# GpSimd is allowed to make the staged weights' sums and low parts in a one-core window attention with two feed-forward layers

## The chip, the cores and the metric

The kernel runs on one core of a Trainium2 chip, as one program. The metric is the device time of one execution in microseconds; lower is better. The engines are named as the profile names them: PE is TensorE (PEld its weight loads), DVE is VectorE, ACT is ScalarE, POOL is GpSimd, SP is SyncE, which here issues every DMA. Each engine works through its own queue of instructions in order, and waits at an instruction until the semaphores that it needs have arrived.

## The reference, cut to what matters

Four sequences of 576 tokens with 8 heads of 64 columns go through causal attention with a window of 64; the result, 2304 tokens by 512 columns, goes through two feed-forward layers with 2048 hidden columns.

```python
scores = scale * np.matmul(q, k.transpose(0, 1, 3, 2))
mask = (rel >= 0) & (rel < window)
...
x = np.ascontiguousarray(attn_out.transpose(0, 2, 1, 3)).reshape(B * S, H * D)
# layer 1
h = x @ w_in
r = np.maximum(h, 0.0)
x = (s * (r * r) + b) @ w_out
# layer 2
h = x @ w_in
g = np.maximum(h, 0.0) + alpha * np.minimum(h, 0.0)
return (g @ w_out).astype(np.float32)
```

## The kernel before

**Numbers in two parts.** A weight or an activation `a` is kept as a high part (a copy to fp32r, `hi`) and a low part (`a - hi`, `lo`), and a product is three matmuls: high by high, high by low, low by high. The function `pair` makes both parts: the copy runs on ACT (in some places DVE may take it), the subtraction on DVE.

**Fewer products.** For most of both layers, two blocks of 128 hidden columns are multiplied together by a scheme with seven block products in place of eight (`hidden_pair`, `product`). It needs, beside the weights themselves, four sums of weight halves. `weight_pair` makes these for the input weights of a pair of hidden blocks, and `out_pair` makes the like for four pairs of output weights: each converts two weight blocks from the 64-bit input (`converted`: ACT lines 668 and 672, DVE lines 677 to 687), makes four sums of 128x256 (`adds`, lines 765 to 768 and 1133 to 1136, into the tile `as__86`), and calls `pair` on the blocks and on the sums. A row with the name `raw` as input is a converted block, one with `as__86` a sum.

**Staging.** Two of the 13 input pairs are written straight into the weight area `aw` (`direct`). The other 11, and all four output pairs, are made ahead of time in the tiles `ag` (now and then `as__86`), stored to the DRAM tensors `wd` and `vd` (SP lines 788 and 1148) and loaded again when their turn comes (lines 809 and 1115). Inputs `x` go the same way through `xd` (stores line 823, loads line 941).

**What PE does with it.** A pair's seven products share PSUM banks: product 1 writes bank `h`, ACT copies it to a bank of `ab` (line 989), product 6 goes on in that copy, which is copied again for product 7, and once more into an `h` bank for product 4. PE has projections (line 1419, `y`) to do between these, and the order in PE's queue is fixed. If a copy is late, PE stands still at the next dependent product.

**What sets the order.** The class `Plan` records every piece of work as a step with the engines that may do it, an assumed cost for each, what it reads and writes, and a due time. `emit` then plays the steps through with these assumed costs, picks for each step the engine on which it would end soonest (weighted by `SPARE`), and issues instructions in that order. An order once issued is fixed; on the chip only the semaphores decide when an instruction starts. The assumed costs of this case:

```python
def act(cols, fn):
    return ("act", 0.2 + cols * 0.00084, fn, 0.0)
...
def dve(cols, fn, fast=False, port=False):
    return ("dve", 0.15 + cols * (0.00053 if fast else 0.00106), fn, 0.0) + (True,) * (fast or port)
...
def pool(cols, fn):
    return ("pool", 0.1 + cols * 0.00184, fn, 0.0)
```

A DVE step with the fifth entry `True` is charged 0.8 of the time by which it would overlap a POOL step.

Of the kernel before, what the change touches and what calls it, by code (L numbers as in the profile page):

```python
# [58 lines left out]
def f32(ap):  # L59
    return ap.bitcast(F32)  # L60
# [188 lines left out]
def tile_window_attention_two_mlps(  # L249
# [74 lines left out]
# [5 lines that stand above are left out]
# [28 lines left out]
    with tc.manual_schedule():  # L357
# [334 lines left out]
        def pair(cols, src, hi, lo, reads, keys, at, after=0.0, either=True):  # L692

            ways = [act(cols, lambda: nc.scalar.copy(hi(), src()))]
            if either == 2 or either and at < PAIRS_ACT:
                ways.append(dve(cols, lambda: nc.vector.tensor_copy(hi(), src()), fast=True))
            T.step(ways, reads=reads, writes=[k + "h" for k in keys], at=at, after=after)
            T.step(
                [dve(cols, lambda: nc.vector.tensor_sub(lo(), src(), f32(hi())), port=True)],  # L699
                reads=reads + [k + "h" for k in keys], writes=[k + "l" for k in keys], at=at, after=after,  # L700
            )
# [54 lines left out]
        def weight_pair(n, layer, f1, f2, at, after, direct):  # L756
# [7 lines left out]
            def adds():  # L764
                nc.vector.tensor_add(sv(0), a(1, 0), a(1, 1))
                nc.vector.tensor_sub(sv(2), a(0, 0), a(1, 0))
                nc.vector.tensor_sub(sv(1), sv(0), a(0, 0))
                nc.vector.tensor_sub(sv(3), a(0, 1), sv(1))
# [3 lines left out]
            def stage(k, s, reads):  # L772
# [11 lines left out]
                pair(cols, s, lambda: v(0), lambda: v(1), reads, keys, at, after)  # L784
# [8 lines left out]
            T.step([("dve", 1.75, adds, 0.0, True)], reads=ts, writes=[sums_], at=at, after=after)  # L793
# [326 lines left out]
        def out_pair(k, at, after):  # L1120
# [11 lines left out]
            def adds():  # L1132
                nc.vector.tensor_add(sv(0), a(1, 0), a(1, 1))
                nc.vector.tensor_sub(sv(2), a(0, 0), a(1, 0))
                nc.vector.tensor_sub(sv(1), sv(0), a(0, 0))
                nc.vector.tensor_sub(sv(3), a(0, 1), sv(1))
# [3 lines left out]
            def stage(lo, hi, s, reads):  # L1140
# [5 lines left out]
                pair(cols, s, lambda: half(0), lambda: half(1), reads, [key], at, after)  # L1146
# [8 lines left out]
            T.step([("dve", 1.75, adds, 0.0, True)], reads=ts, writes=[sums_], at=at, after=after)  # L1155
# [519 lines left out]
```

## Time and profile before

| what | value |
|---|---|
| median of three runs | 842.25 us (841.49 to 843.48) |
| the profiled execution | 840.98 us, of which the span is 839.2 us |
| PE, PEld busy | 824.7 us (98%), 775.7 us (92%) |
| DVE, ACT, POOL busy | 693.1 us (83%), 536.9 us (64%), 106.1 us (13%) |
| granted TensorE clock | 1.0 throughout |

The span runs from the first to the last instruction. Busy times are sums over one engine's instructions; since matmuls are pipelined, a short pause between two of them does not show as idle time of PE, and the idle time of PEld is the better measure of it.

### The profile page before, as it was taken

The numbers are of one execution on the slowest core, as the hardware profiler recorded it, in microseconds if no ns is written. First come the engines' busy times: TensorE is split into PE (matmuls) and PEld (weight loads), VectorE is DVE, ScalarE is ACT, GpSimd is POOL, SyncE is SP. The second block draws the span as 40 slices with busy tenths as digits, with TensorE's granted clock in tenths as the row PEclk, the third lists the DMA queues.
The fourth block names the chain that finished last, engine by engine and source line by source line (L and its number), as shares of the span: only waits on it lengthen the run. The fifth ranks groups of instructions, "written<-read, shape, count | busy, mean of one in ns | idle before, by whom it ended". The sixth has DMA issues, their size and how long they took to land.

```text
span 839.2 us, 15002 instructions
## 1 busy us (share of the span) xinstructions
PE 824.7 (98%) x5517; PEld 775.7 (92%) x5521; DVE 693.1 (83%) x1210; ACT 536.9 (64%) x1219; POOL 106.1 (13%) x117
## 2 busy tenths in 40 slices
PE   8899999999999999999999999999999999999997
PEld 4678878888899999999999999999999999999997
DVE  6978799698987887699888999878888688778695
ACT  6878997554676555477648678778655345445461
POOL 6443344442011010011000000000000000000000
PEclk9999999999999999999999999999999999999999
DMA  8576974467558989958799668858998667438813
GB/s 287 183 229 176 297 222 131 184 235 284 212 204 314 376 312 316 411 186 339 282 382 380 227 248 309 320 183 303 345 389 314 230 225 268 123 121 338 319 42 109
DMA packets 72648, 217.25 MB, mean 259 GB/s; under 512 B 7424, under 2 KB 25984, under 8 KB 72576
## 3 DMA queue, kind: packets, MB, share of 16 engines
q1 hardware_dynamic: 72576, 216.31, 71.8%
q8 instruction: 43, 0.70, 0.3%
q14 instruction: 29, 0.24, 0.1%
HBM read 151.00 MB, written 65.27 MB: 258 GB/s over the span
## 4 chain that ended last, share of the span: by engine, by line
PE 76%; DVE 10%; DMA 6%; ACT 3%; POOL 3%; issue 1%; SPq 0%; DVEq 0%; POOLq 0%; ACTq 0%
PE y L1419 23%; PE h L978 17%; PE ab L978 13%; PE y L1218 11%; DMA raw<-w_in 3%; PE h L1336 3%; DMA xd<-aq 3%; PE y L1396 3%; PE y L628 2%; PE y L597 2%; PE ab L523 1%; DVE aq L699 1%; ACT as__86 L562 1%; POOL as__86 L580 1%; DVE ag L1051 1%
## 5 line engine op out<-in xcount | busy, mean ns | idle before, releaser
L1419 PE MATMUL y<-ax,woh 128*128 128x384 f32 x864 | 196.2, 334 | 0.0
L978 PE MATMUL h<-ax,aw 128*128 128x384 f32 x936 | 184.4, 334 | 0.7 <-ACT h L989 0.6
L978 PEld LDWEIGHTS h<-ax,aw 128*128 128x128 f32 x936 | 164.2, 188 | 1.6 <-ACT h L989 0.9
L1419 PEld LDWEIGHTS y<-ax,woh 128*128 128x128 f32 x864 | 153.7, 188 | 0.5 <-DVE ay L1496 0.3
L978 PE MATMUL ab<-ax,aw 128*128 128x384 f32 x702 | 139.7, 335 | 1.1 <-ACT h L989 0.9
L978 PEld LDWEIGHTS ab<-ax,aw 128*128 128x128 f32 x702 | 123.1, 188 | 2.4 <-ACT h L989 1.6
L1419 PE MATMUL y<-ax,wol 128*128 128x384 f32 x432 | 121.2, 334 | 0.0
L1336 PE MATMUL h<-ax,aw 128*128 128x512 f32 (+1 forms) x360 | 83.9, 377 | 1.1 <-DVE ax L646 1.1
L1419 PEld LDWEIGHTS y<-ax,wol 128*128 128x128 f32 x432 | 79.0, 188 | 0.0
L1336 PEld LDWEIGHTS h<-ax,aw 128*128 128x128 f32 x360 | 62.0, 189 | 12.8 <-DVE ax L646 1.5
L1051 DVE TENSOR_TENSOR ax<-r,ax 128x384 fp32r<-128x384 f32 x108 | 57.9, 553 | 5.7 <-ACT ax L1048 5.2
L668 ACT ACTIVATE raw<-raw 128x512 f32<-128x512 f32 x64 | 43.2, 679 | 28.8 <-DMA raw<-w_in 16.5
L1006 DVE TENSOR_TENSOR aq<-ab,aq 128x768 f32<-128x768 f32 x39 | 37.3, 955 | 15.7 <-PE ab L978 11.9
L1062 ACT ACTIVATE r<-r 128x384 f32<-128x384 f32 (+2 forms) x90 | 47.5, 543 | 1.1
L580 POOL TENSOR_TENSOR as__86<-as__86,den 128x512 f32<-128x512 f32 x36 | 40.3, 1142 | 56.2 <-DVE den L573 34.1
L682 DVE SCALAR_TENSOR_TENSOR raw<-raw 128x512 int32<-128x512 int32 x64 | 46.3, 725 | 1.2 <-ACT raw L672 1.2
L1058 ACT ACTIVATE r<-h 128x384 f32<-128x384 f32 (+2 forms) x57 | 29.7, 521 | 27.4 <-PE h L1336 17.6
L1499 DVE TENSOR_TENSOR ay<-y,ay 128x384 f32<-128x384 f32 x72 | 37.7, 553 | 9.6 <-PE y L1419 9.5
L733 POOL TENSOR_TENSOR wsum<-wsum,raw 128x512 f32<-128x512 f32 x15 | 21.9, 1459 | 181.6 <-DVE raw L687 180.1
L687 DVE CUSTOM_DVE_ANT_0 raw<-raw 128x1024 uint16<-128x1024 uint16 x64 | 44.7, 704 | 0.1
L672 ACT ACTIVATE raw<-raw 128x512 int32<-128x512 uint32 x64 | 43.0, 680 | 2.4 <-DMA raw<-w_in 1.6
L1218 PE MATMUL y<-ax,woh 128*128 128x384 f32 (+1 forms) x183 | 41.3, 333 | 0.6 <-ACT y L1232 0.6
(164 smaller groups left out, 1493.7 us busy)
## 6 DMA issues: line engine op xcount, KB each, us to landing
ax<-xd SPq DMA_DIRECT2D x91, 768.0 KB, 6.3
aw<-wd SPq DMA_DIRECT2D x33, 512.0 KB, 5.1
raw<-w_in SPq DMA_DIRECT2D x32, 512.0 KB, 6.9
raw<-w_out SPq DMA_DIRECT2D x32, 512.0 KB, 5.5
xd<-ax SPq DMA_DIRECT2D x21, 768.0 KB, 4.5
wd<-ag SPq DMA_DIRECT2D x30, 512.0 KB, 6.6
xd<-aq SPq DMA_DIRECT2D x12, 768.0 KB, 4.1
xd<-ax SPq DMA_DIRECT2D x36, 192.0 KB, 4.6
```

Source lines behind the costliest of these rows:

```text
L580: eng.tensor_mul(x, x, d)
L668: [act(512, lambda: nc.scalar.activation(T[t], H().bitcast(F32), AF.Abs, scale=65536.0))],
L672: [act(512, lambda: nc.scalar.activation(L(), L().bitcast(U32), AF.Copy, scale=2.0 ** -29))],
L682: [dve(512, lambda: nc.vector.scalar_tensor_tensor(out=L(), in0=H(), scalar=-0x80000000, in1=L(), op0=ALU.bitwise_and, op1=ALU.bitwise_or) ...
L687: [dve(512, lambda: nc.vector.tensor_tensor(ti(), ti(), L(), op=ALU.add), port=True)],
L978: nc.tensor.matmul(bank(), W[:, wj, a, kt * P:(kt + 1) * P], X[:, c, kt, :], start=start and kt == 0 and y == 0, stop=kt == 1 and y == 2, ...
L1051: [dve(n, lambda: nc.vector.tensor_sub(T[gl], rn(), f32(T[gh])), port=True)],
L1062: [act(n, lambda: nc.scalar.activation(rn(), rn(), AF.Square)), dve(n, lambda: nc.vector.tensor_mul(rn(), rn(), rn()), port=True)],
L1218: nc.tensor.matmul(v(to)[:, c], W[:, s, a * P:(a + 1) * P], G[:, h, c], start=start and p == 0 and y == 0, stop=p == 1 and y == 2, skip_gr ...
L1336: nc.tensor.matmul(T[ps][:, :n].rearrange("p (c t) -> p c t", t=P), T[w][:, k * P:(k + 1) * P], T[X(x, k)], start=st, stop=sp,)
L1419: nc.tensor.matmul(ps, T[w][:, m * P:(m + 1) * P], T[x], start=(i == 0 and j == 0), stop=(last and j == 2), skip_group_check=closing(layer ...
L1499: ways = [dve(n, lambda a=a, yn=yn: nc.vector.tensor_add(a(), yn(), a()))]
```

## The change

`pair` gets an argument `spare`; where it is true, the low part may also be made by GpSimd. `weight_pair` sets it for staged pairs, `out_pair` always, and in both the four sums may be made by GpSimd too, at an assumed cost of 2.4 us for all four against 1.75 us on DVE. Nothing is computed differently; which engine takes a step is decided by `emit`.

```diff
-        def pair(cols, src, hi, lo, reads, keys, at, after=0.0, either=True):
+        def pair(cols, src, hi, lo, reads, keys, at, after=0.0, either=True, spare=False):
...
             T.step(
-                [dve(cols, lambda: nc.vector.tensor_sub(lo(), src(), f32(hi())), port=True)],
+                [dve(cols, lambda: nc.vector.tensor_sub(lo(), src(), f32(hi())), port=True)]
+                + [pool(cols, lambda: nc.gpsimd.tensor_sub(lo(), src(), f32(hi())))] * spare,
...
-            def adds():
-                nc.vector.tensor_add(sv(0), a(1, 0), a(1, 1))
-                nc.vector.tensor_sub(sv(2), a(0, 0), a(1, 0))
-                nc.vector.tensor_sub(sv(1), sv(0), a(0, 0))
-                nc.vector.tensor_sub(sv(3), a(0, 1), sv(1))
+            def adds(eng):
+                eng.tensor_add(sv(0), a(1, 0), a(1, 1))
+                eng.tensor_sub(sv(2), a(0, 0), a(1, 0))
+                eng.tensor_sub(sv(1), sv(0), a(0, 0))
+                eng.tensor_sub(sv(3), a(0, 1), sv(1))
...
-                pair(cols, s, lambda: v(0), lambda: v(1), reads, keys, at, after)
+                pair(cols, s, lambda: v(0), lambda: v(1), reads, keys, at, after, spare=not direct)
...
-            T.step([("dve", 1.75, adds, 0.0, True)], reads=ts, writes=[sums_], at=at, after=after)
+            T.step([("dve", 1.75, lambda: adds(nc.vector), 0.0, True)] + [("pool", 2.4, lambda: adds(nc.gpsimd), 0.0)] * (not direct),
+                   reads=ts, writes=[sums_], at=at, after=after)
...
-                pair(cols, s, lambda: half(0), lambda: half(1), reads, [key], at, after)
+                pair(cols, s, lambda: half(0), lambda: half(1), reads, [key], at, after, spare=True)
...
-            T.step([("dve", 1.75, adds, 0.0, True)], reads=ts, writes=[sums_], at=at, after=after)
+            T.step([("dve", 1.75, lambda: adds(nc.vector), 0.0, True), ("pool", 2.4, lambda: adds(nc.gpsimd), 0.0)],
+                   reads=ts, writes=[sums_], at=at, after=after)
```

The issued order shows which instructions moved. Counted over the program, 123 instructions leave DVE for POOL: 41 low parts of 128x512 (two times 256 columns), 22 low parts of 128x256, and 60 sums of 128x256 (four each for 11 input pairs and 4 output pairs). Beside these, a handful of small steps change between ACT and DVE. PE has the same 4941 matmuls and SP the same 440 DMAs as before. The order of every engine is the same up to about the first staged pair and, for PE, again over its last 1050 or so matmuls. Line numbers of the changed kernel are higher by 1 from line 700, by 2 from line 795 and by 3 from line 1158.

First, DVE at the first staged input pair, before; line 699 is a low part, 765 to 768 the four sums, 1051 a low part of an activation that PE will read:

```order
L687 ISA raw<-raw 128x1024
L699 TENSOR_TENSOR ag<-raw,ag 128x2x256
L765 TENSOR_TENSOR as__86<-raw 128x256
L766 TENSOR_TENSOR as__86<-raw 128x256
L767 TENSOR_TENSOR as__86<-as__86,raw 128x256
L768 TENSOR_TENSOR as__86<-raw,as__86 128x256
L1051 TENSOR_TENSOR ax<-r,ax 128x384
L1006 TENSOR_TENSOR aq<-ab,aq 128x768
L1051 TENSOR_TENSOR ax<-r,ax 128x384
L699 TENSOR_TENSOR ag<-as__86,ag 128x2x256 x2
```

The same place on DVE in the change:

```order
L687 ISA raw<-raw 128x1024
L682 SCALAR_TENSOR_TENSOR raw<-raw 128x512
L1053 TENSOR_TENSOR ax<-r,ax 128x384
L687 ISA raw<-raw 128x1024
L1053 TENSOR_TENSOR ax<-r,ax 128x384
L1008 TENSOR_TENSOR aq<-ab,aq 128x768
L1061 TENSOR_SCALAR r<-aq 128x384
L742 SCALAR_TENSOR_TENSOR wol_2966<-raw,s_sb,woh_2954 128x512
```

The low parts and sums are gone from DVE, and conversion and activation work closes up. On POOL, where there was a run of `wsum` additions before, the change has, at the first staged pairs:

```order
L700 TENSOR_TENSOR ag<-raw,ag 128x2x256
L766 TENSOR_TENSOR as__86<-raw 128x256
L767 TENSOR_TENSOR as__86<-raw 128x256
L768 TENSOR_TENSOR as__86<-as__86,raw 128x256
L769 TENSOR_TENSOR as__86<-raw,as__86 128x256
L734 TENSOR_TENSOR wsum<-wsum,raw 128x512
L700 TENSOR_TENSOR ag<-as__86,ag 128x2x256 x2
L700 TENSOR_TENSOR ag<-raw,ag 128x256
```

So POOL gets eight instructions for one staged input pair. The consumer of the sums is ACT, which casts them to their high parts. Its queue at the same place, with the semaphores that each waits for, before (line 989 is the copy between PSUM banks that PE waits for):

```order
L989 COPY h<-ab 128x384 [waits PE_49,Activation_49]
L1048 CAST ax<-r 128x384 [waits Activation_49]
L694 CAST ag<-as__86 128x2x256 [waits DVE_49] x2
L1058 ACTIVATE r<-aq 128x384 [waits DVE_49] x2
L1062 ACTIVATE r<-r 128x384 [waits Activation_49] x2
L989 COPY ab<-h 128x384 [waits PE_49]
```

And in the change:

```order
L991 COPY h<-ab 128x384 [waits PE_49,Activation_49]
L1050 CAST ax<-r 128x384 [waits Activation_49]
L694 CAST ag<-as__86 128x2x256 [waits Pool_49] x2
L694 CAST ag<-raw 128x256 [waits DVE_49]
L739 ACTIVATE woh_2954<-raw,s_sb 128x512 [waits DVE_49]
L1060 ACTIVATE r<-aq 128x384 [waits DVE_49]
```

The two casts keep their place in ACT's queue, but now wait for POOL.

## Rows read from the trace of the kernel before

**Rows 1.** The page: span, and part 1 (busy time, share, instructions).

```profile
span 839.2 us, 15002 instructions
PE 824.7 (98%) x5517; PEld 775.7 (92%) x5521; DVE 693.1 (83%) x1210; ACT 536.9 (64%) x1219; POOL 106.1 (13%) x117
```

**Rows 2.** Windows: stretch, its length, busy us per engine, clock, DMA share, GB/s.

```profile
60.00:245.00 185.00, 184.93 (x1468) 154.14 (x1467) 160.37 (x244) 131.69 (x341) 63.21 (x52) 1.00 0.65 213
245.00:655.00 410.00, 408.84 (x2355) 407.11 (x2354) 344.09 (x658) 274.55 (x547) 11.61 (x11) 1.00 0.83 311
```

**Rows 3.** Waits of PEld, 245 to 655 us: total us, times, longest.

```profile
PEld ab L978 <- ACT h L989: 1.6, 2, 1.2
PEld h L978 <- ACT r L1058: 0.4, 1, 0.4
PEld ab L978 <- ACT ab L989: 0.4, 1, 0.4
PEld y L1419 <- DVE ay L1496: 0.3, 1, 0.3
```

**Rows 4.** Chain that ended last, 340 to 360 us: start, length, what.

```profile
345.48 0.32 SPq L788
...
345.86 10.63 DMA raw<-w_in
...
357.73 0.39 ACT h L989
```

**Rows 5.** Waits of ACT, 245 to 655 us.

```profile
ACT raw L668 <- DMA raw<-w_in: 11.3, 7, 4.0
...
ACT raw L668 <- DMA raw<-w_out: 9.5, 6, 2.8
```

**Rows 6.** DVE groups by form, 245 to 655 us: busy us, mean ns | idle before.

```profile
L699 DVE TENSOR_TENSOR ag<-as__86,ag 128x512 fp32r<-128x512 f32 x26 | 17.1, 685 | 0.3 <-ACT ag L694 0.3
...
L699 DVE TENSOR_TENSOR ag<-raw,ag 128x256 fp32r<-128x256 f32 x23 | 9.4, 419 | 0.0
...
L768 DVE TENSOR_TENSOR as__86<-raw,as__86 128x256 f32<-128x256 f32 x11 | 4.7, 425 | 0.4
...
L1136 DVE TENSOR_TENSOR as__86<-raw,as__86 128x256 f32<-128x256 f32 x4 | 1.7, 425 | 0.1
```

**Rows 7.** POOL group by form, 245 to 655 us.

```profile
L733 POOL TENSOR_TENSOR wsum<-wsum,raw 128x512 f32<-128x512 f32 x7 | 10.2, 1454 | 138.2 <-DVE raw L687 138.1
```

**Rows 8.** Timeline of POOL: start, us, what.

```profile
148.99 1.98 POOL L873 TENSOR_TENSOR as__86<-ax 128x384 f32<-128x384 f32 x2 [4.30 <-DVE aq L883]
...
225.94 1.67 POOL L733 TENSOR_TENSOR wsum<-wsum,raw 128x512 f32<-128x512 f32 x1 [22.86 <-DVE raw L687]
...
234.92 1.30 POOL L733 TENSOR_TENSOR wsum<-wsum,raw 128x512 f32<-128x512 f32 x1 [2.15 <-DVE raw L687]
```

**Rows 9.** Timeline of DVE around the last two rows of POOL.

```profile
225.77 0.69 DVE L699 TENSOR_TENSOR aw<-as__86,aw 128x512 fp32r<-128x512 f32 x1
226.42 1.74 DVE L1051 TENSOR_TENSOR ag<-r,ag 128x512 fp32r<-128x512 f32 x1
...
234.69 2.48 DVE L1462 TENSOR_TENSOR ay<-y,ay 128x512 f32<-128x512 f32 x4
```

**Rows 10.** Timeline of DVE and of ACT at the first staged pair.

```profile
245.27 0.69 DVE L699 TENSOR_TENSOR ag<-raw,ag 128x512 fp32r<-128x512 f32 x1
...
249.62 1.14 ACT L694 CAST ag<-as__86 128x512 fp32r<-128x512 f32 x2
```

**Rows 11.** Waits of SP's queue, 245 to 655 us.

```profile
SPq L809 <- PE ab L978: 32.3, 10, 6.9
SPq L809 <- PE h L978: 26.3, 20, 5.2
SPq L788 <- DVE ag L699: 18.1, 14, 4.0
```

**Rows 12.** Waits of DVE, 245 to 655 us.

```profile
DVE ay L1499 <- PE y L1419: 9.5, 9, 3.3
DVE aq L1006 <- PE ab L978: 9.4, 13, 3.3
```

More of the change, by code (lines that the diff above doesn't have):

```diff
@@ L1130, in out_pair, with adds @@
             sv = lambda j: T[sums_][:, j * W2:(j + 1) * W2]
[L1132 to L1136, printed above, removed]
+            def adds(eng):
+                eng.tensor_add(sv(0), a(1, 0), a(1, 1))
+                eng.tensor_sub(sv(2), a(0, 0), a(1, 0))
+                eng.tensor_sub(sv(1), sv(0), a(0, 0))
+                eng.tensor_sub(sv(3), a(0, 1), sv(1))
             x3 = lambda ap: ap.rearrange("p (x c) -> p x c", c=W2)
```

## The prediction

> **What bounds the kernel now.** I read part 1 of the page first: PE is busy for 825 of 839 us, its weight loads for 776, and no other engine comes near [rows 1]. Then I cut the span at the places where the change begins and ends. The staged weight pairs are made from about 245 to 655 us; the order of instructions before that, and PE's order behind it, are the same in both kernels. In these 410 us the weight loads, which show short pauses better than the matmuls do, are busy for 407.1 us [rows 2]. So PE pauses for 2.9 us there, and the same 4941 matmuls have to go through PE after the change, at the granted clock of 1.00 that it has already. **No rearrangement in this stretch can gain more than about 2.9 us, 0.34% of the time.**
>
> The third view is who ends these pauses. Four kinds of waits make up 2.7 us, and three of them, 2.4 us, name ACT; DVE is named once, with 0.3 us [rows 3]. The chain of waits around the longest shows what held ACT: SP issued a staging store, then the load of a raw weight, which landed 10.6 us after its start; ACT stood at the first conversion of that weight, and the copy that PE needed was behind it in ACT's queue [rows 4]. ACT waited so for raw weights for 20.8 us in 13 waits [rows 5], and 2.4 us of that arrived at PE: **about 0.115 us of PE's time per us of such a wait.** This ratio is an estimate from these two sets of rows (it charges all of ACT's share of PE's waits to them); I use it below as the price of a blocked queue.
>
> **What the change takes from DVE.** 41 low parts of 128x512 at 0.685 us, 22 of 128x256 at 0.419, and 60 sums at 0.425, the mean of the last of each four, which is the dearest [rows 6]: 28.1 + 9.2 + 25.5 = 62.8 us, all inside the stretch. DVE's 344.1 us there [rows 2] become 281. That is off the path: PE waited for DVE for 0.3 us. I credit this 0.3 us. The ends are 0, if the freed time only makes DVE wait elsewhere, and 2.9, if all pauses of PE went. The few steps that change between ACT and DVE are one or two 384-column instructions either way in 410 us, and I set them to nothing; ACT, busy for 274.6 of 410 us, covers them.
>
> **What it gives to POOL.** A two-input instruction of 128x512 takes 1.454 us on POOL in the stretch [rows 7], so 41 of these are 59.6 us. A 128x256 one is not in the trace. The nearest rows: two of 128x384 in 1.98 us, and the shortest 128x512 shown at 1.30 [rows 8], which is 0.31 us for 128 columns and leaves 0.68 for 256; with the hindrance of the 512 ones (1.454 over 1.30) it is 0.76, and 82 of them 62 us. The bounds are half of 1.30 and the whole 0.99, so 53 to 81 us. POOL gains some 122 us and stands at 228 in the whole run, at 134 of 410 us (33%) in the stretch. It has room.
>
> **What POOL's work costs DVE.** At 225.94 us POOL adds to `wsum` for 1.67 us [rows 8]; the DVE subtraction that begins inside it, at 226.42, takes 1.74 us, where one of the same size right before took 0.69 [rows 9]. It was held for 1.05 us, nearly to the end of POOL's instruction. At the other end, the four DVE additions with one input in PSUM from 234.69 us take 0.62 us each [rows 9] while POOL's addition from 234.92 takes its shortest 1.30 [rows 8]: nothing. So POOL's 122 us cost DVE between 0 and 63% of themselves (1.05 over 1.67); I take the middle, 0.36 of 122, or 44 us, because DVE's rows are a mix of both kinds. **Of the 62.8 us freed, some 19 are left**, and DVE ends at 325 of 410 us, 281 to 358.
>
> The Trainium skill, page "SBUF — State Buffer", section "Who interferes with whom", says that a DVE instruction with two SBUF inputs and a GpSimd instruction that reads SBUF share a read interface, which is an exclusive lock for the whole instruction: the second to start is fully blocked. By that rule the row at 226.42 is the normal case and the rows from 234.69 are the exempt one, and the trace agrees with both. Were all of DVE's work of the blocked kind, the whole 122 us would come back to DVE; that is the last rival below.
>
> What does DVE's holding cost PE? The nearest stretch is 60 to 245 us: POOL is busy there for 63.2 of 185 us, 34%, DVE for 160.4, 87%, and PE idles for 0.07 us [rows 2]. That is the load that the change brings, and scaled to 410 us it costs 0.2 us. But most of that stretch lacks the chain of copies between dependent products. With the price of a blocked queue, 77 us of holding would be 8.9 us at most. I take 0.4, near the first, since it shows the same engines under the same load.
>
> **What it costs ACT.** The two casts of sums keep their place in ACT's queue and now wait for POOL; behind them stand the copies for PE. At the first staged pair the low part began on DVE at 245.27 and ACT's cast ran at 249.62 [rows 10]. On POOL one low part and four sums take 1.454 + 4 x 0.76 = 4.49 us, so they end at 249.76 and ACT is held for 0.14. The planner assumed 1.04 + 2.4 = 3.44 us for these five; where it put the cast right behind, ACT stands for the missing 1.05 us. With 15 staged pairs that is 2 to 16 us of waiting; I take 9, the middle, which at 0.115 is 1.0 us for PE (0.2 to 1.8).
>
> The staging stores wait for the low parts on POOL, which come later than they did, but nothing waits for the data soon: the loads back from DRAM (line 809) wait for PE to leave the weight area, for 58.6 us in total, while the stores wait for DVE's low parts for 18.1 us [rows 11]. The cover is gone only for what is queued behind a store on SP, which is the second rival.
>
> **Sum.** -0.3 + 0.4 + 1.0 = +1.1 us on the profiled execution's 840.98 us (span 839.2 and 1.8 around it): 842.1. That execution lies 1.3 us under the median of the runs, 842.25, so in their terms I say **843.3 us**.
>
> **The rivals.** About 0.2% (1.7 us) is what a measurement of this kernel can tell from no change.
>
> *No change, 842 to 844* (the forecast), chance 0.48: PE full before and after. For it speaks the 60 to 245 us stretch.
>
> *SP's queue passes the delay on, slower*, chance 0.33. One staged input pair is 3 x 1.454 + 5 x 0.76 = 8.2 us on POOL against 3 x 0.685 + 4 x 0.425 + 0.419 = 4.2 on DVE. Its stores go out some 4 us later, and behind them in SP's queue stand raw weight loads, as in the chain of waits around 345 us [rows 4]. The planner allowed 3 x 1.04 + 2.4 + 0.57 = 6.1 us, so 2.1 us per pair, 31 us for 15, are not in its order. If all 31 reach ACT, PE loses 3.6 us more, and if the whole 15 x 4 = 60 do, 6.9. Price: 847 us, up to 850. It decides, by more than 1.7 us, from 15 us of added waiting on. Against it: only some stores have a raw load behind them, and not every one is needed at once.
>
> *The relief shows, faster*, chance 0.14. At least 2 of PE's 2.9 us of pauses go, because DVE returns its results sooner, and no new ones come: 840.2 us. Against it: the pauses name ACT and late raw weights, which the change does not touch.
>
> *DVE becomes the bound, slower*, chance 0.05. All 122 us of POOL's time block DVE: 281 + 122 = 403 us of work. It cannot fill its waits for PE's results, 18.9 us [rows 12], so the stretch needs 422 us: 12 more, 854 us. The exempt rows speak against it.
>
> **Range and chances.** Low 839.9: the faster rival, with a little noise. High 849: the forecast's terms at their upper ends, and the SP rival up to most of its price. Left out are the DVE rival (0.05), the top of the SP rival (0.07) and the bottom of the faster one (0.05). Faster by over 0.2%: 0.14. Within 0.2%: 0.48. Slower: 0.33 + 0.05 = 0.38.
>
> **What would show it.** POOL's busy time near 228 us, its 512-column instructions near 1.45 and its 256-column ones near 0.76; DVE between 631 and 707 us in all, near 674; DVE instructions over 1 us where their kind takes 0.4 to 0.7. PE's weight loads in 245 to 655 us should still be busy for 405 us or more; ACT should list waits of its casts (line 694) for POOL of 2 to 16 us. If ACT's waits for raw weights grow from 20.8 us to 36 or more and PE's waits for line 989 with them, the SP rival is right. If PE pauses for under 1.2 us in the stretch, the relief was real. I am wrong altogether if the time moves while PE's pauses there don't.

## The result, and the profile after

The change takes 853.89 us (median of 5 runs, 852.66 to 856.45) against 842.25 us for the kernel before (5 runs on the same chip, 840.26 to 843.48): a ratio of 1.0147, 95% interval 1.0121 to 1.0174. It is 1.5% slower; 843.3 was predicted, and 853.89 lies above the range. The execution profiled after took 852.66 us, its span 850.2.

The page of the changed kernel, span and part 1, which answers to [rows 1]:

```profile
span 850.2 us, 15084 instructions
...
PE 829.9 (98%) x5521; PEld 775.7 (91%) x5521; DVE 681.1 (80%) x1085; ACT 536.3 (63%) x1221; POOL 235.5 (28%) x240
```

POOL gained 129 us, DVE lost only 12, and PE's weight loads are busy for the same 775.7 us as before in a span that is 11 us longer. So the time went into pauses of PE. The windows say where, as in [rows 2]:

```profile
60.00:245.00 185.00, 184.69 (x1466) 153.99 (x1466) 160.10 (x244) 131.25 (x340) 63.91 (x53) 1.00 0.65 212
245.00:655.00 410.00, 401.65 (x2288) 395.08 (x2288) 326.78 (x521) 269.19 (x539) 140.31 (x134) 1.00 0.83 307
```

From 60 to 245 us nothing moved. From 245 to 655 us the weight loads are busy for 395.1 us instead of 407.1: they pause for 14.9 us where they paused for 2.9, and these 12.0 us are the loss (the span is 11.0 us longer). The granted clock is 1.00 there as before. Who ends the pauses (waits of PEld in this stretch, as in [rows 3]):

```profile
PEld h L980 <- ACT r L1060: 4.6, 4, 1.9
PEld h L980 <- DVE r L1080: 3.8, 5, 1.6
PEld ab L980 <- ACT h L991: 1.4, 3, 0.7
PEld y L1422 <- DVE ay L1499: 1.1, 3, 0.4
```

They are many and short. In the largest two groups PE waits for an `h` bank which ACT (line 1060) or DVE (line 1080) has yet to read into `r`; before, the first was 0.4 us [rows 3] and the second wasn't there. Five smaller groups, 3.5 us together, are left out. What POOL's new instructions take, by form, in the same stretch:

```profile
L700 POOL TENSOR_TENSOR ag<-as__86,ag 128x512 fp32r<-128x512 f32 x26 | 37.7, 1466 | 5.9 <-ACT ag L694 3.6 <-issue 1.9 <-DVE ag L696 0.4
L700 POOL TENSOR_TENSOR ag<-raw,ag 128x256 fp32r<-128x256 f32 x22 | 18.6, 856 | 45.6 <-ACT ag L694 28.7 <-DVE ag L696 11.9 <-DVE ax L1053 5.0
...
L768 POOL TENSOR_TENSOR as__86<-as__86,raw 128x256 f32<-128x256 f32 x11 | 9.9, 903 | 0.0
```

What became of DVE's remaining instructions:

```profile
L1053 DVE TENSOR_TENSOR ax<-r,ax 128x384 fp32r<-128x384 f32 x102 | 67.0, 672 | 6.0 <-ACT ax L1050 5.7
...
L1502 DVE TENSOR_TENSOR ay<-y,ay 128x384 f32<-128x384 f32 x64 | 33.6, 550 | 18.5 <-PE y L1422 18.5
...
L677 DVE TENSOR_SCALAR raw<-raw 128x512 f32<-128x512 f32 x42 | 24.8, 591 | 13.7 <-ACT raw L668 13.7
L1008 DVE TENSOR_TENSOR aq<-ab,aq 128x768 f32<-128x768 f32 x26 | 24.8, 953 | 13.7 <-PE ab L980 13.1 <-ACT h L991 0.6
...
L1080 DVE SCALAR_TENSOR_TENSOR r<-aq,side 128x384 f32<-128x384 f32 x22 | 15.3, 738 | 0.6 <-ACT aq L1077 0.5
L1080 DVE SCALAR_TENSOR_TENSOR r<-h,side,aq 128x384 f32<-128x384 f32 x23 | 14.0, 609 | 2.2 <-ACT aq L1077 2.2
```

Line 1080 shows the pattern in itself: with both tensors in SBUF it takes 738 ns, with one (`h`) in PSUM 609. Before the change both forms took the same, and the low part that is now line 1053 took 553 ns instead of 672:

```profile
L1051 DVE TENSOR_TENSOR ax<-r,ax 128x384 fp32r<-128x384 f32 x105 | 56.3, 553 | 5.7 <-ACT ax L1048 5.2
...
L1078 DVE SCALAR_TENSOR_TENSOR r<-h,side,aq 128x384 f32<-128x384 f32 x24 | 14.7, 613 | 5.6 <-ACT aq L1075 5.6
L1078 DVE SCALAR_TENSOR_TENSOR r<-aq,side 128x384 f32<-128x384 f32 x24 | 13.8, 614 | 0.1
```

Two more views say who stands at POOL's results. ACT:

```profile
ACT raw L668 <- DMA raw<-w_in: 12.5, 8, 2.7
ACT raw L668 <- DMA raw<-w_out: 5.2, 4, 2.7
...
ACT raw L668 <- POOL as__86 L769: 3.1, 2, 2.4
ACT ag L694 <- POOL as__86 L768: 2.8, 3, 1.7
ACT ag L694 <- POOL as__86 L769: 1.3, 3, 0.6
```

With three smaller rows ACT waits for POOL for 9.9 us. Its waits for raw weights fell, from 20.8 us [rows 5] to 17.7. SP's stores wait for POOL longer than they waited for DVE; its queue, as in [rows 11], the store of an input pair and that of an output pair:

```profile
SPq L789 <- POOL ag L700: 51.1, 23, 6.7
...
SPq L1150 <- POOL ag L700: 24.0, 16, 5.3
```

Before, the first was 18.1 us [rows 11], and the second:

```profile
SPq L1148 <- DVE ag L699: 14.3, 10, 5.5
```

The place of PE's longest pause, in the timelines of DVE, POOL, ACT and PEld (start, us, what):

```profile
411.68 1.79 DVE L687 CUSTOM_DVE_ANT_0 raw<-raw 128x1024 uint16<-128x1024 uint16 x1
...
413.84 0.85 DVE L678 TENSOR_SCALAR raw<-raw 128x512 int32<-128x512 int32 x1
414.61 1.22 DVE L682 SCALAR_TENSOR_TENSOR raw<-raw 128x512 int32<-128x512 int32 x1
...
411.63 1.30 POOL L700 TENSOR_TENSOR ag<-raw,ag 128x512 fp32r<-128x512 f32 x1 [3.42 <-ACT ag L694]
413.62 0.79 POOL L766 TENSOR_TENSOR as__86<-raw 128x256 f32<-128x256 f32 x1 [0.69 <-DVE raw L687]
...
416.51 0.92 POOL L769 TENSOR_TENSOR as__86<-raw,as__86 128x256 f32<-128x256 f32 x1
...
417.46 0.67 ACT L668 ACTIVATE raw<-raw 128x512 f32<-128x512 f32 x1 [2.37 <-POOL as__86 L769]
418.04 0.46 ACT L1060 ACTIVATE r<-h 128x384 f32<-128x384 f32 x1
...
418.56 0.47 PEld L980 LDWEIGHTS h<-ax,aw 128*128 128x128 f32 x3 [1.94 <-ACT r L1060]
```

Read it backwards. PE waits 1.94 us for ACT's line 1060, which empties an `h` bank. That instruction was behind a conversion (line 668), which stood 2.37 us for POOL's last sum, because the sum reads the `raw` buffer that the conversion overwrites. The sums began late because DVE's line 687, which finishes the raw weight, took 1.79 us beside POOL's low part instead of 0.69. So two things are tangled here: DVE is held, and queues stand at POOL's late results.

### The profile page after: what moved, and what is told of

Read it like the earlier page. It is cut to its first block, busy times and chain, and to the rows that moved or that the text cites. A ratio compares the mean times of both kernels' runs of the same rounds, so it can differ in the third digit from the quotient of the medians.

```text
span 850.2 us, 15084 instructions
## 1 busy us (share of the span) xinstructions
PE 829.9 (98%) x5521; PEld 775.7 (91%) x5521; DVE 681.1 (80%) x1085; ACT 536.3 (63%) x1221; POOL 235.5 (28%) x240
## 4 chain that ended last, share of the span: by engine, by line
PE 56%; DVE 19%; DMA 11%; POOL 5%; ACT 5%; issue 3%; SPq 0%; DVEq 0%; POOLq 0%; ACTq 0%
PE y L1422 13%; PE h L980 12%; PE y L1221 10%; PE ab L980 9%; DMA xd<-aq 4%; DMA raw<-w_in 3%; PE h L1339 3%; DMA raw<-w_out 3%; PE y L1399 3%; DVE raw L677 2%; DVE raw L682 2%; DVE ax L1053 2%; PE y L628 2%; DVE raw L687 2%; PE y L597 2%
## 5 line engine op out<-in xcount | busy, mean ns | idle before, releaser
L980 PE MATMUL h<-ax,aw 128*128 128x384 f32 x936 | 186.4, 336 | 6.9 <-ACT r L1060 3.3
L700 POOL TENSOR_TENSOR ag<-raw,ag 128x256 fp32r<-128x256 f32 (+1 forms) x32 | 34.7, 1092 | 180.2 <-ACT ag L694 160.6
L1053 DVE TENSOR_TENSOR ax<-r,ax 128x384 fp32r<-128x384 f32 x108 | 70.2, 665 | 6.8 <-ACT ax L1050 6.5
L668 ACT ACTIVATE raw<-raw 128x512 f32<-128x512 f32 x64 | 43.1, 676 | 32.1 <-DMA raw<-w_in 19.1
L682 DVE SCALAR_TENSOR_TENSOR raw<-raw 128x512 int32<-128x512 int32 x64 | 52.3, 818 | 6.1 <-ACT raw L672 6.1
L677 DVE TENSOR_SCALAR raw<-raw 128x512 f32<-128x512 f32 x64 | 37.9, 591 | 13.7 <-ACT raw L668 13.7
L687 DVE CUSTOM_DVE_ANT_0 raw<-raw 128x1024 uint16<-128x1024 uint16 x64 | 47.3, 740 | 0.2
```

Of the source, the lines that this page charges most:

```text
L668: [act(512, lambda: nc.scalar.activation(T[t], H().bitcast(F32), AF.Abs, scale=65536.0))],
L677: nc.vector.tensor_scalar(T[t], T[t], W_MIN, W_MAX, op0=ALU.max, op1=ALU.min)
L682: [dve(512, lambda: nc.vector.scalar_tensor_tensor(out=L(), in0=H(), scalar=-0x80000000, in1=L(), op0=ALU.bitwise_and, op1=ALU.bitwise_or) ...
L687: [dve(512, lambda: nc.vector.tensor_tensor(ti(), ti(), L(), op=ALU.add), port=True)],
L980: nc.tensor.matmul(bank(), W[:, wj, a, kt * P:(kt + 1) * P], X[:, c, kt, :], start=start and kt == 0 and y == 0, stop=kt == 1 and y == 2, ...
L1053: [dve(n, lambda: nc.vector.tensor_sub(T[gl], rn(), f32(T[gh])), port=True)],
```

## The experiments

Three theories. **Hold:** POOL's instructions that read SBUF hold DVE's, whose results come late to PE. **Waits:** the planner's costs for POOL are too low, so ACT and SP stand at POOL's late results. **Order:** the new order is worse by itself. "The loss" is the median minus that of the kernel before on the same chip. The ratio comes with an interval, and isn't always that of the medians. DVE, POOL and PEld are busy times of the profiled execution, PEld in 245 to 655 us.

| run | loss, us | ratio (95%) | DVE | POOL | PEld |
|---|---|---|---|---|---|
| the kernel before | | | 693.1 | 106.1 | 407.1 |
| **the change** | 11.6 | 1.0147 (1.0121 to 1.0174) | 681.1 | 235.5 | 395.1 |
| 1, moved work back on DVE, order kept | 3.9 | 1.0039 (1.0024 to 1.0054) | 691.7 | 106.3 | 401.9 |
| 2, before + idle reading on POOL | 37.3 | 1.0454 (1.0402 to 1.0506) | 757.3 | 246.5 | 377.3 |
| 3, before + idle fills on POOL | 1.8 | 1.0008 (0.9993 to 1.0024) | 698.5 | 247.6 | 405.9 |
| 4, planned with true costs | 8.4 | 1.0106 (1.0073 to 1.0139) | 680.0 | 238.9 | 398.6 |
| 5, fills in place | 0.9 | 1.0011 (0.9988 to 1.0034) | 643.7 | 218.2 | 406.6 |
| 6, one column in place | 0.4 | 1.0006 (0.9987 to 1.0024) | 640.2 | 138.3 | 407.9 |
| 7, sums only | 1.2 | 1.0020 (1.0001 to 1.0040) | 687.7 | 160.5 | 406.0 |
| 8, low parts only | 7.4 | 1.0089 (1.0058 to 1.0120) | 692.6 | 190.1 | 398.7 |
| 9, in pieces of 128 columns | 19.6 | 1.0253 (1.0226 to 1.0280) | 664.3 | 286.6 | 390.8 |
| 10, fills as long as 9 | 32.1 | 1.0380 (1.0338 to 1.0422) | 646.9 | 291.8 | 383.6 |
| 11, fills as long as the change | 4.6 | 1.0055 (1.0037 to 1.0074) | 644.1 | 230.1 | 401.5 |
| 12, run 2 with half the columns | 3.9 | 1.0046 (1.0028 to 1.0065) | 718.3 | 201.1 | 403.5 |
| 13, run 4 with fills | 3.4 | 1.0046 (1.0029 to 1.0063) | 642.6 | 229.5 | 404.3 |
| 14, hold in one stretch per pair | 7.0 | 1.0089 (1.0062 to 1.0116) | 667.7 | 223.8 | 397.7 |
| 15, the same readings, spread | 1.6 | 1.0014 (1.0002 to 1.0027) | 654.6 | 219.8 | 404.8 |
| 16, readings as long as the change's | 14.7 | 1.0187 (1.0160 to 1.0213) | 672.1 | 247.9 | 393.5 |
| 17, run 16 with fills | 4.8 | 1.0060 (1.0042 to 1.0078) | 644.5 | 236.6 | 402.1 |

### Runs 1 to 4: a first separation

**Run 1.** The planner still thinks that the work is on POOL, but DVE gets it.

```diff
-                + [pool(cols, lambda: nc.gpsimd.tensor_sub(lo(), src(), f32(hi())))] * spare,
+                + [pool(cols, lambda: nc.vector.tensor_sub(lo(), src(), f32(hi())))] * spare,
...
-[("pool", 2.4, lambda: adds(nc.gpsimd), 0.0)]
+[("pool", 2.4, lambda: adds(nc.vector), 0.0)]
```

> The change's plan and order are kept, but the moved low parts and sums are issued on VectorE, at the place where the plan put GpSimd's. Theory 1 (GpSimd's instructions that read SBUF hold VectorE's instructions with two SBUF inputs, and PE gets its results late): the hold is gone, VectorE has its 62.8 us back, 842 to 847 us, its 128x384 low parts of activations near 550 ns again where the change shows 665. Theory 2 (the planner's costs for GpSimd are too low, so queues stand at GpSimd's results): those waits are gone, about 842 to 845. Theory 3 (the order that came out is worse by itself, on whatever engine the work is): 850 us or more, weight loads still some 15 us short in the stretch from 245 to 655 us.

846.25 us. Two thirds of the loss went with POOL's share; line 1053 is back at 575 ns. Not clean for the order: here DVE does 123 instructions that the plan didn't leave room for.

**Run 2.** The kernel before, and for each staged low part and sum POOL also subtracts finished tiles of the same size into a scratch tile.

```diff
+            nc.gpsimd.tensor_sub(out, x, y)
```

> The kernel before with its order and all its work, and beside it on GpSimd, for each staged low part and each of the sums, a subtraction of the same size that reads the finished tiles into a scratch tile; nothing waits for its result. Theory 1: VectorE is held as in the change and is not relieved of anything, so 850 to 862 us, with VectorE's 128x384 low parts of activations at 650 ns or more. Theory 2 and theory 3: nothing waits for GpSimd and the order is that of before, so 842 to 844 us.

879.64 us, far above the range. Hardly anything waits for these instructions (0.2 us on ACT from 245 to 655 us, nothing on PE, DVE and SP) and the order is that of before, so a hold alone can cost more than the whole change. The 64 us by which DVE's busy time grew became 37 us for PE; the change relieves DVE, this run doesn't.

**Run 3.** The same places, but one column is copied (to set the time) and the rest of the time is fills.

```diff
+            nc.gpsimd.tensor_copy(out[:, :1], at)
+            for _ in range(2):
+                nc.gpsimd.memset(out, 0.0)
```

> As the kernel before with extra work on GpSimd that nobody waits for, but the extra instructions only write: for each staged low part and each sum a copy of one column (which only sets the time) and two fills of the same number of columns. Theory 1: filling reads nothing, so VectorE is not held: 842 to 845 us, with its 128x384 low parts of activations near 553 ns. Should any busy GpSimd slow VectorE, reading or not, 848 us or more, as far as GpSimd's added time comes near the change's 129 us. Theories 2 and 3: 842 to 844 us.

844.13 us: not to be told from no change, with POOL busy for 247.6 us. A POOL that is busy but reads next to nothing costs nothing that can be told here; a reading POOL does.

**Run 4.** POOL is the only choice, and the planner knows what it takes there.

```diff
+                [("pool", 0.86 if cols == 256 else 1.47, lambda: nc.gpsimd.tensor_sub(lo(), src(), f32(hi())), 0.0)] if spare else
...
-[("pool", 2.4, lambda: adds(nc.gpsimd), 0.0)]
+[("pool", 3.5, lambda: adds(nc.gpsimd), 0.0)]
```

> The change with all of the staged low parts and sums on GpSimd as the only choice, and the planner told what they take there: 1.47 us for 512 columns, 0.86 for 256, 3.5 for four sums. Theory 1: the hold on VectorE stays, 849 to 856 us. Theory 2: the order now leaves room for GpSimd's real times, the waits for GpSimd's results on ACT, 10 us in the change, shrink, and most of the loss is gone: 843 to 846 us. Theory 3: unclear, a new order.

850.68 us. ACT's waits for POOL shrank from 9.9 us to 1.5 and a quarter of the loss went with them; most stayed.

### Runs 5, 6, 10 and 11: POOL's time without the hold

All have the change's plan and order. **Run 6** reduces each moved instruction to one column. **Runs 5, 11 and 10** put fills between a first and a last instruction of one column, so that results come as late as if they were computed: 1.36, 1.50 and 2.5 us for a low part of 512 columns (the sums of their groups' means).

```diff
-nc.gpsimd.tensor_sub(lo(), src(), f32(hi()))
+low1(lo(), src(), f32(hi()), cols)
...
+        def low1(lo, src, hi, cols):
+            nc.gpsimd.tensor_copy(caps.rearrange("p x c -> p (x c)")[:, :2].bitcast(F32), one(hi))
+            spend(*((2, 395) if cols == 512 else (1, 222)))
+            nc.gpsimd.tensor_sub(one(lo), one(src), one(hi))
```

Here `one` is a column and `spend` so many fills of so many columns (run 11's; run 5 has 2 of 330 and 1 of 112, run 10 has 4 of 428 and 2 of 300).

> The change's plan and order, but each of the moved instructions computes one column only on GpSimd, some 0.3 us each (the other columns of the staged low parts and sums are left out). Neither hold nor long waits are left. Theory 1 and theory 2: 839 to 843 us. Theory 3 (the order is worse by itself): 846 us or more.

843.1 us, no change. Its window, as in [rows 2], and two of its groups on DVE, the twins of the change's lines 1053 and 677:

```profile
245.00:655.00 410.00, 408.90 (x2358) 407.88 (x2358) 291.70 (x534) 273.64 (x549) 43.86 (x134) 1.00 0.83 311
...
L1062 DVE TENSOR_TENSOR ax<-r,ax 128x384 fp32r<-128x384 f32 x105 | 57.5, 564 | 12.3 <-ACT ax L1059 11.7
...
L677 DVE TENSOR_SCALAR raw<-raw 128x512 f32<-128x512 f32 x42 | 18.8, 449 | 13.8 <-ACT raw L668 13.7
```

This says two things: the order isn't worse by itself, and **even when the moved work costs nearly nothing on POOL, freeing DVE of it gains nothing**. DVE has 52.4 us less to do in the stretch (291.7 against 344.1), and PE's weight loads are busy for 407.9 us against 407.1.

> The change's plan and order, GpSimd at the same places for about the same time, and everything that waited for it still waits; but its time is spent in fills, which read nothing, and of each low part and sum only one column is computed (so the rest of the low parts and sums is left out). Theory 1 (GpSimd's reading instructions hold VectorE, and PE gets late): the hold is nearly gone and VectorE keeps its relief, 840 to 844 us. Theory 2 (queues stand at GpSimd's results): nothing is gained, 849 to 856 us. Both in parts: between, and the place between says how much is whose.

843.58 us, which read like a clean win for the hold. It wasn't: POOL was at 218 us where the change has 235, and its results came earlier than the change's. From start to end, the short gaps between fills included, its low parts of 512 columns took 1.50 us on average, those of 256 columns 0.69 and four sums 3.19, where the change has 1.50, 0.86 and 3.47 (means over the timelines of POOL).

> As the run with fills in GpSimd's places, with the fills made longer so that a low part of 512 columns takes 1.47 us, one of 256 0.86 and four sums 3.5, as in the change (one column of each low part and sum is computed). Theory 1 (the hold): still 840 to 845 us. Theory 2 (queues stand at GpSimd's late results): if the 15% that the fills were short decide, 849 us or more.

847.32 us. With 12 us more on POOL the waits alone lose 4.6, with hardly any hold (line 1053's twin is at 563 ns, as with one column, and DVE is busy for 644.1 us against 640.2). So the waits theory has a part, which the first runs had hidden. Counted as for run 5, its results took 1.61, 0.84 and 3.65 us, somewhat longer than the change's: the change lies between runs 5 and 11. Run 11's window, and its twins of lines 1053 and 678:

```profile
245.00:655.00 410.00, 405.12 (x2323) 401.45 (x2322) 294.80 (x531) 273.85 (x550) 135.99 (x376) 1.00 0.84 312
...
L1072 DVE TENSOR_TENSOR ax<-r,ax 128x384 fp32r<-128x384 f32 x107 | 58.6, 563 | 13.6 <-ACT ax L1069 13.1
...
L678 DVE TENSOR_SCALAR raw<-raw 128x512 int32<-128x512 int32 x42 | 20.9, 498 | 1.4
```

> The same with fills as long as the run in pieces took: 2.5 us, 1.3 and 4.3 (one column of each is computed). Theory 1 alone: 840 to 845 us, although everything that waits for GpSimd waits for as long as in the run in pieces, 862 us. Theory 2, above some point: 855 us or more, and then the run in pieces lost its time by waits for GpSimd and not by the hold on VectorE.

874.75 us. Lateness alone can cost more than the whole change, too. Not all of the 32.1 us is waiting: in five stretches, 20 us together, the granted clock was at its lower level (1.2 GHz, 0.50 in the rows), each time in or right behind a pause of PE of 1.3 to 4.9 us. The 56 weight loads in these stretches took 0.325 us each instead of 0.175, some 8 us more in all. In the change's profile the clock stays at 1.00. ACT's waits for POOL in run 11 and in run 10, in the same stretch:

```profile
ACT ag L713 <- POOL as__86 L708: 10.2, 8, 2.7
...
ACT raw L668 <- POOL as__86 L709: 3.1, 2, 2.2
```

```profile
ACT ag L713 <- POOL as__86 L708: 16.3, 7, 3.9
...
ACT raw L668 <- POOL as__86 L709: 7.8, 2, 5.7
...
ACT raw L668 <- POOL caps L697: 4.8, 2, 4.6
```

### Runs 7, 8 and 9: parts and pieces

**Run 7** leaves the low parts on DVE (no `spare`), **run 8** the sums (no `pool` way for `adds`), **run 9** cuts POOL's instructions into pieces of 128 columns.

```diff
-                pair(cols, s, lambda: v(0), lambda: v(1), reads, keys, at, after, spare=not direct)
+                pair(cols, s, lambda: v(0), lambda: v(1), reads, keys, at, after)
...
```

```diff
-            T.step([("dve", 1.75, lambda: adds(nc.vector), 0.0, True)] + [("pool", 2.4, lambda: adds(nc.gpsimd), 0.0)] * (not direct),
+            T.step([("dve", 1.75, lambda: adds(nc.vector), 0.0, True)],
...
```

```diff
+            for x in range(0, cols, P):
+                nc.gpsimd.tensor_sub(cut(lo, x), cut(src, x), cut(hi, x))
...
```

> The change for the sums alone: the low parts stay on VectorE. GpSimd gets some 53 us instead of 129. Theory 1, by the size of the hold: about 40% of the loss, 845 to 849 us. Theory 2: the wait for the four sums was what stopped ScalarE at the longest pause, so most of the loss stays: 848 to 853 us.

843.88 us: below both ranges, and at the edge of what can be told.

> The change for the low parts alone, the sums stay on VectorE: some 75 us for GpSimd. Theory 1, with a price that grows with the hold (sums alone: 20 us of hold, 1.7 us lost; the change: 51 and 11.6): 844 to 849 us. Theory 2: the sums' late arrival is what stops ScalarE, so 842 to 844 us here.

850.07 us, just above the hold's range, where the waits theory wanted no loss. The two parts lose 1.2 + 7.4 = 8.6 of the 11.6 us.

> The change, but GpSimd does each of its moved instructions in pieces of 128 columns, two to four in a row, same plan and order. Theory 1, if VectorE is held for the rest of one GpSimd instruction at most: single holds get shorter (the longest VectorE instructions of 128x384 under 1 us), in total about the same or, with gaps between pieces, less; 845 to 853 us. Theory 2: each piece has its own fixed part, so GpSimd's results come later, 855 us or more.

862.28 us. DVE is held less than in the change (664.3 us busy against 681.1), but 128 columns take 0.51 to 0.64 us in all but the rarest group, so POOL needs 51 us more. Run 10, whose fills were meant to take these times, lost more still, but there the moved work takes 205 us from start to end, against 182 here. So lateness alone can cost as much as the pieces did; how much of run 9's loss is the hold stays open. Pieces don't help.

### Runs 12 and 13: a smaller hold, and the order of true costs

**Run 12** is run 2 with half the columns in each repeated instruction; **run 13** is run 4 with run 11's fills.

```diff
-            nc.gpsimd.tensor_sub(out, x, y)
+            nc.gpsimd.tensor_sub(half(out), half(x), half(y))
```

> As the run with extra reading subtractions that nobody waits for, each of half the columns: some 75 us of GpSimd in place of 129. Theory 1, if PE loses in proportion to the hold (64 us of hold cost 37): hold 35 us, 20 us lost, 862 us. If VectorE's idle time takes the first part of a hold: less than in proportion, 847 to 856 us. Theory 2: 842 to 844 us.

846.62 us, a little under the range: DVE grew by 25 us, PE lost 3.9. With run 2 (64 us, 37.3): the first part of a hold is cheap, then it isn't.

> The order with GpSimd's true costs (850.7 us), with fills of the same length in GpSimd's places: one column of each low part and sum is computed, nothing holds VectorE. If the hold is what that order lost: 841 to 844 us. If the order itself, or what is left of its waits for GpSimd, lost it: 848 us or more.

845.79 us, outside both ranges. The true-cost order loses 3.4 us without a hold and 8.4 with it, so 5.0 are the hold's.

### Runs 14 to 17: a hold without waits, in the change's order

POOL computes one column of each moved instruction, so that its results are early, and then reads a scratch tile that nobody waits for. **Run 14** does all the reading behind the last result of a pair, **run 15** behind several, **run 16** the same with as many columns as the change reads, and **run 17** replaces run 16's readings by two fills each.

```diff
+        def pay():
+            while owed:
+                x = caps.rearrange("p x c -> p (x c)")[:, :2 * owed.pop()].bitcast(F32)
+                nc.gpsimd.tensor_sub(x, x, x)
...
+            nc.gpsimd.tensor_sub(one(lo), one(src), one(hi))
+            owed.append(416 if cols == 512 else 160)
+            if last:
+                pay()
```

```diff
-            owed.append(416 if cols == 512 else 160)
+            owed.append(cols)
...
-            owed.extend((432, 432))
+            owed.extend((512, 512, 256))
```

```diff
-                nc.gpsimd.tensor_sub(x, x, x)
+                nc.gpsimd.memset(x, 0.0)
+                nc.gpsimd.memset(x, 0.0)
```

> The change's plan and order. GpSimd computes one column of each moved instruction (the rest is left out), so that nothing waits long for it, and only after the last of a staged pair it does subtractions on a scratch tile that nobody waits for, reading for about as long as the change's instructions took. So VectorE is held and no queue waits. If the hold is a cause of its own: VectorE 25 to 50 us longer than in the run with one column (640 us), and 847 to 852 us. If the waits for GpSimd are the whole cause: 842 to 844 us, as with one column.

849.4 us, as the hold theory says. But 2.9 us of it is one pause of PE, while ACT stood 4.9 us for an addition to `wsum` that was queued behind 6 us of reading. The row of ACT's waits:

```profile
ACT raw L668 <- POOL wsum L757: 4.9, 1, 4.9
```

> As the run with a hold and no waits, but the readings that nobody waits for are spread over the staged pair, right behind GpSimd's results, in place of one run of 6 us at its end, so that hardly anything waits behind them (one column of each moved instruction is computed). VectorE is held for some 27 us. If the hold is a cause by itself: 845 to 848 us. If what was lost before was that one wait: 842 to 844 us.

843.85 us, in the range of the second answer, though the interval of the ratio lies just above 1. Spread out, the same readings hold DVE for 14 us only (654.6 against run 6's 640.2), not 27.

> The same with readings as long as the change's instructions were in all (512, 256, and 1280 columns for four sums), so that VectorE is held for about 41 us, as in the change. If the change's loss is the hold's part and the waits' part (4.6 us) added up: 847 to 850 us. If hold and waits only lose together: 842 to 845 us.

856.9 us, more than expected, with DVE held for 32 us; no row of ACT's waits names POOL. The two kinds of stores wait for POOL's low parts here as long as in the change (51.7 and 25.3 us), so the lateness of those had to be told apart. PE's two longest pauses, and what ACT did before the first of them:

```profile
PEld y L1445 <- ACT ax L1073: 2.7, 1, 2.7
PEld h L1003 <- DMA ax<-xd: 2.4, 1, 2.4
...
567.66 0.65 ACT L672 ACTIVATE raw<-raw 128x512 int32<-128x512 uint32 x1 [2.56 <-DMA raw<-w_out]
568.22 0.49 ACT L1073 CAST ax<-r 128x384 fp32r<-128x384 f32 x1
...
569.30:572.70 3.40, 3.14 (x10) 3.14 (x11) 1.03 (x3) 2.22 (x6) 0.00 (x0) 0.50 0.00 0
```

Both end with a load from DRAM that came late. The last row shows the granted clock at its lower level for 3.4 us right behind the first of them, with 11 weight loads done where a stretch just before (560 to 566 us) has 35 in 6.0 us.

> The run that reads as much as the change (856.9 us), with each reading replaced by two fills of the same columns, so that GpSimd is busy for as long and at the same places, its results and the stores behind them come as late, but VectorE isn't held (one column of each moved instruction is computed). If the hold on VectorE is what lost the 14.7 us: 842 to 846 us. If it was the lateness of GpSimd's results and of the stores: 852 us or more.

847.02 us, between the two. Runs 16 and 17 have the same order; one reads and the other writes. From start to end the readings take 110.4 us together, the fills 110.7 (156.5 and 150.3 with the one-column instructions). Their windows, run 16 first:

```profile
245.00:655.00 410.00, 399.58 (x2272) 393.54 (x2271) 316.62 (x521) 268.73 (x539) 151.71 (x240) 1.00 0.82 304
```

```profile
245.00:655.00 410.00, 405.55 (x2327) 402.13 (x2326) 295.26 (x531) 274.49 (x551) 142.34 (x350) 1.00 0.83 311
```

DVE is busy for 21 us more with reading beside it, and PE's weight loads for 8.6 us less. ACT's busy time over the whole run is the same (535.3 and 535.6 us).

**What follows.** Three pairs of runs differ only in whether POOL reads or fills: the change and run 11 (11.6 and 4.6 us lost), run 4 and run 13 (8.4 and 3.4), run 16 and run 17 (14.7 and 4.8). Reading costs 7.0, 5.0 and 9.9 us more, and what is left without it, 3.4 to 4.8 us, is lateness of POOL's results. **The hold on DVE is the larger part of the loss, some 7 of 11.6 us, the late results the rest; the order by itself costs nothing.** The split has an uncertainty of some 3 us, from the intervals of the runs. POOL's busy time is 5 to 11 us shorter with fills, but that is the gaps between them: from start to end, the moved work takes 130 us in the change, 137 in run 11 and 122 in run 5, 135 and 134 in runs 4 and 13. So the fills' results are about as late on average, though not the same from one instruction to the next (four sums take 2.9 to 4.6 us in the change). The change lies between run 5, which loses 0.9 us, and run 11, so its hold may be worth more than 7.0. The third pair's 9.9 is 8.0 between the two profiled executions; the other four of run 16 have a mean granted clock of 0.992 to 0.994 against 0.998 in the profiled one, so some of its loss is time at the lower clock.

What stays open is which of the late results makes up the rest. In run 11 ACT waits for POOL for 14.3 us. In run 17 it does so for 1.0, with stores that wait for their data about as long (81 us against 88 in run 11, all rows of the stores to `wd` and `vd`). ACT's waits for the data of raw weights are 26.5 us there and 28.0 in run 16 (four rows, lines 668 and 672), where the kernel before has 22.9, run 6 19.9 and the change 20.0. Run 17's longest pause of PE, 1.4 us, ends as run 16's longest does, behind a conversion that stood 2.5 us for a raw weight, and the loads of these weights stand in SP's queue behind output stores that waited for POOL. So in runs 16 and 17 a delay does seem to pass through SP's queue, with reading and without. No run was made to part the two.

## Why the prediction was wrong

**What bounds the kernel: right.** PE had 2.9 us to give, and run 6's time shows nothing of DVE's relief: of the term of -0.3 us nothing can be told from 0.

**What leaves DVE: too large, without effect.** 62.8 us were summed from single durations; run 6 frees 52.4. Instructions that follow each other overlap in the records (in the change's trace line 682 at 409.61 for 0.69 us, the next at 410.21), so a sum of durations is more than the time that comes free: in the trace of before, DVE's busy time without the moved instructions is 51.5 us less.

**What POOL gets: right, a little short.** 129 us against 122; 1.466 us for most instructions of 512 columns against 1.454, 0.86 on average for 256 columns (0.77 to 0.96 by group) against 0.76.

**What DVE is held: right.** 681.1 us in the change against 640.2 in run 6, which has the same order, is 41 us; 44 were predicted. The middle of the prediction's own ends, 0 and 63%, would have been 0.315 and 38 us, not 0.36; the 41 us are 0.32 of POOL's 129. The rows named next are of the kinds which the Trainium skill, page "SBUF — State Buffer", section "Who interferes with whom", names as contending with GpSimd: two inputs in SBUF, or a one-input form with two ports such as a tensor_scalar. The rows agree: line 1053 goes from 564 ns in run 6 to 672 and the tensor_scalar of line 677 from 449 to 591, while lines 1502 and 1008, which read one input from PSUM, stay at 550 and 953.

**What the hold costs PE: the step that failed.** I took 0.4 us, "near the first, since it shows the same engines under the same load": the stretch from 60 to 245 us, where PE idles for 0.07 us beside a POOL at 34%. The runs measure some 7 us for 41 us of hold. The load was indeed the same, and DVE was held there as well. In the trace of before, from 60 to 245 us:

```profile
L1051 DVE TENSOR_TENSOR ag<-r,ag 128x512 fp32r<-128x512 f32 x24 | 20.5, 856 | 2.2 <-ACT ag L1048 2.2
...
L677 DVE TENSOR_SCALAR raw<-raw 128x512 f32<-128x512 f32 x16 | 10.5, 656 | 0.0
```

An instruction of the first's size took 0.69 us [rows 9]; the second takes 0.449 in run 6 and 0.591 in the change. What differed is the dependences: in the later stretch an `h` bank has to be emptied into `r` by ACT or DVE before PE can go on, and the two largest groups of waits, 8.4 us, name just that. This is argued from who ends PE's pauses; no run tests it. The prediction had said of that earlier stretch that "most of that stretch lacks the chain of copies between dependent products", and then took its number anyway. The 0.07 us was also the wrong view: it is idle time of PE, which hides short pauses. PE's weight loads waited there for DVE for 0.5 us, still little. The other end, 8.9 us from the price of a blocked queue, holds the 7. The range was to reach up to "the forecast's terms at their upper ends"; with 8.9 and 1.8 us these give 853, four above the 849 that was stated.

**What ACT's waits cost: about right in length, wrong in price.** 9 us of waiting at the casts were predicted; 6.8 came there, and 3.1 at line 668. At 0.115 us each the 9 were 1.0 us; run 11, with 14.3 us of such waits and later stores, loses 4.6. The price was read from waits that PE could mostly absorb, and longer waits cost more: run 10 has 32.2 us of them, in the three rows shown and one of 3.3, and loses 32.1, with some 8 of these at the lower clock. So two terms were too small, the hold's by more than 6 us and this one by up to 3.6.

**The rivals.** SP's queue did get its added waiting, 75 us for the two kinds of stores instead of 32, but in the change it doesn't show where the rival put it: ACT's waits at line 668 for raw weights fell to 17.7 us. In runs 16 and 17 its path shows. The rival that DVE becomes the bound has the measured time, 854, by another mechanism: it wanted DVE at its limit, and DVE is busy for 327 of the 410 us, less than before. DVE wasn't too busy; it was late at single places, and in an order fixed in advance PE had no other work to do at those.

## What to carry to other kernels

Before moving work off an engine that isn't the bound, make that work nearly free in a trial (one column of each instruction) and time it: here that gains nothing, so in this order even a perfect GpSimd would not have won. Take the price of a delay from a stretch with the same dependences, not from one with the same load: where a chain through a few banks feeds PE, a us of DVE's hold cost PE 0.1 to 0.6 us. It is no fixed price even in one order: 41 us cost some 7 in the change, 32 us 9.9 in run 16. To tell a hold from a wait, keep the other engine's time and replace its reading by filling; compare the two from start to end, since busy time leaves out the gaps between fills.

## What was not expected of the hardware

Fills on POOL leave DVE's two-input instructions alone (563 ns for 128x384 in run 11, 564 in run 6), but lengthen its tensor_scalar of line 678 from 428 ns in run 6 to 498 in run 11. In the Trainium skill, page "SBUF — State Buffer", section "Who interferes with whom", two-port forms contend with GpSimd in general and two-input ones with its reads only; the rows fit that.

The loss isn't in proportion to the hold. In the order of before, 25 us of it cost 3.9 us and 64 us cost 37.3; in the change's order, spread out, 14 us cost 1.6 and 32 us cost 14.7 (4.8 of that without the hold).

POOL seems to be held too: its low part of 128x512 took 1.466 us on average and 1.611 where it reads `raw`, against 1.30 for the one shown at 411.63. And small instructions are dear there: one column of a two-input instruction takes 0.19 to 0.37 us (means of groups in runs 6 and 11), so that four pieces of 128 columns (0.60 us each) take 2.4 us where one of 512 takes 1.47.
